# Weight loads and transposed pieces in the first feed-forward quarter of a transformer block on one core: another order in SyncE's queue, and one chunk of the next input split per block

## The chip, the cores and the metric

The kernel runs on one core of one Trainium2 chip. The metric is the device time of one execution in microseconds (us). The kernel before was timed three times: 1166.69, 1166.88 and 1167.59 us, a median of 1166.88 us. One more execution was taken by the hardware profiler; all rows quoted below are of that one, and their times count from its first instruction.

## What is computed

A pre-norm transformer block on x of 1 x 2048 x 448 in float32: grouped attention of 16 heads (width 28) with one key and value head, then a gated feed-forward of width 1792.

```python
x = A_x
h = x + _A_ref(_layernorm(x), A_wq, A_wk, A_wv, A_wo)   # attention
h2 = h + _B_ref(_layernorm(h), B_w1, B_w3, B_w2)
# _B_ref(x): gate = x @ w1; up = x @ w3; out = (silu(gate) * up) @ w2
```

## The kernel before

**Stages.** The rows of x are cut into four quarters of 512 (`NT = 4`). Attention runs up to 739 us of the span; from there the feed-forward runs quarter by quarter, and this text is about that. The order of all instructions on all engines is the order in which the program is written (a manual schedule); each engine then works through its own list strictly in turn, and semaphores make it wait where data are missing.

**A block.** One quarter t has 14 blocks k = 0 to 13 (`NF`), each for 128 of the 1792 hidden columns. The main loop (L1132 to L1169) does one block per pass. Weights and inputs are held as a high and a low part, so that three products of reduced precision stand for one in float32. From block (0, 4) on, a block on TensorE (PE) has four pieces in this order: the first half of the two input products of block k (`ffn1_half(..., 0)`), the first half of the w2 product of block k-1 (`ffn2_half(*prev, 0)`), the second half of the input products (`ffn1_half(..., 1)`), and the second half of the w2 product (in `rest`). All go through `two` (line L1025), two 64-row halves of the array at a time.

**Settling.** The two halves of the array change places between first and second half, so a PSUM bank that one has written is then written by the other. `settle` (L1029) keeps them apart: ScalarE (ACT) reads one element of the bank into `pexp`, and PE's next write of that bank waits for this read. In each block ACT does in this order: settle the input products' bank after the first half (PE's second half of the input products waits for it), settle the w2 product's bank (`pexp<-pb`), Silu (L1033), the high part of the hidden value (L1040), whatever `call(t, k)` holds, and the settle of the w2 product's second half (PE's next w2 product waits for it). What `call(t, k + 0.5)` holds comes after that settle and ahead of the next block.

**Weights.** `load_w13(k)` (L175 to L177) issues six DMAs on SyncE's (SP) queue for the columns of block k of w3 and w1, `load_w2(k)` (L184) one. They go to places that attention has left: `W13[6]`, `W13[7]` to `QR3`, `W13[8]`, `W13[9]` to `OT`, `W13[10]` to `W13[13]` to `OS`, the last rows of w2 to `WO`. `split_w(k + 2)` stands at the top of block k: VectorE (DVE) casts (L483), GpSimd (POOL) subtracts (L484). `split_w2(k + 1)` (L496, L497) stands behind the second half of the w2 product. DVE's list of one block is: cast of `W13[k+2]`, product with Silu (L1035), low part of the hidden value (L1041), work of `call(t, k)`, cast of `W2[k+1]`, work of `call(t, k + 0.5)`.

**The next quarter's input.** `ln_norm` and `blocks` (DVE, L213 and L225) norm 128 rows of the next quarter and transpose them in 32 x 32 blocks. What is left to reach the full transposed input is done by DMA: `blocks` puts 16 pieces per 128 rows into a list, and `move(m)` (L238) issues the next m of them on SP. A piece writes 32 partitions and 32 columns of all chunks c of the tile `xh` at once (`to[..., :m, ...]`, m of 4 or 3), so each chunk is whole only when all 64 pieces of a quarter have landed. `split_x(t, c)` (L243, L247) then makes the high and the low part of chunk c: a copy on ACT (two for c = 3) and a subtraction on DVE.

**Where the work stands.** `on(t, k, ...)` puts work into the table that `call` reads, from L1110 to L1129. In the first quarter before: 16 pieces behind block 1, the loads of `W13[8]` and `W13[9]` at 2, of `W13[6]` and `W13[7]` at 2.5, 16 pieces behind block 3, all other loads at 4.5, 16 pieces each behind blocks 5 and 7, chunks 0 and 1 split at 11, chunks 2 and 3 at 12.

Of the kernel before, what the change touches and what calls it, by code (L numbers as in the profile page):

```python
# [35 lines left out]
def block_kernel(  # L36
# [842 lines left out]
    for s in range(AHEAD, LAST):  # L879
        i, c = divmod(s, NC)  # L880
        n, kt = divmod(c, NQ)
# [221 lines left out]
    def on(t, k, fn, *args):  # L1103
        after.setdefault((t, k), []).append((fn, args))
# [10 lines left out]
    for n in range(NQ):  # L1115
        on(0, FULL - 1 + n // 2 / 2, wo_rows, tl, n)
        on(0, 8 + n, ln_stats, tl, n)
    on(0, 4.5, put_late)
    for k in range(8, NF):
        on(0, 2 if k < 10 else 4.5, load_w13, k)  # L1120
        on(0, 4.5, load_w2, k)
    on(0, 12, ln_rstd, tl)
    for t in range(1, NT):
        for n in range(NQ):
            on(t - 1, 1 + 2 * n, ln_norm, t, n)
            on(t - 1, 1 + 2 * n, blocks, t, n)
            on(t - 1, 1 + 2 * n, move, 16)
        on(t - 1, 11, split_x, t, 0, 1)
        on(t - 1, 12, split_x, t, 2, 3)  # L1129

    prev = None
    for t in range(NT):  # L1132
# [68 lines left out]
```

## Time and profile before

| | |
|---|---|
| median of the three runs | 1166.88 us |
| profiled execution: its time, its span | 1165.67 us, 1163.8 us |
| granted TensorE clock, mean | 1.000 |
| PE busy | 1149.7 us (99%) |
| DVE, ACT, POOL busy | 796.9, 765.0, 331.4 us |
| chain that ended last, PE's share | 87% |

A row of the timeline gives start, duration, engine, line, operation, what it writes `<-` what it reads, a count, and in brackets how long the engine had been idle and what ended that. A `q` behind an engine's name (SPq) is its queue of DMA issues: such a row tells of the issue, and the data land later. A row of the windows gives busy time and number of instructions of PE, PE's weight loads (PEld), DVE, ACT and POOL in that stretch, then the granted clock, the share of the DMA engines and GB/s.

### The profile page before, as it was taken

How to read it: one execution, taken by the hardware profiler on the slowest of the kernel's cores; microseconds unless marked ns; L12 is line 12 of the kernel's file. 1: busy time of each engine (PE TensorE's matmuls, PEld its weight loads, DVE VectorE, ACT ScalarE, POOL GpSimd, SP SyncE). 2: the span in 40 equal slices, each digit the busy share in tenths (PEclk: the TensorE clock that was granted, in tenths of full speed). 3: DMA queues.
4: the chain of work that ended last, by engine and by line, in shares of the span. 5: the costliest groups of instructions: out<-in, count | busy, mean ns of one | idle time of the engine just before them, and what ended most of it. 6: DMA issues, size and time to landing. Idle time of an engine off the chain costs nothing.

```text
span 1163.8 us, 25849 instructions
## 1 busy us (share of the span) xinstructions
PE 1149.7 (99%) x10154; PEld 765.9 (66%) x10154; DVE 796.9 (68%) x1498; ACT 765.0 (66%) x1587; POOL 331.4 (28%) x242
## 2 busy tenths in 40 slices
PE   8999999999999999999999999999999999999998
PEld 6664444445444445444445444688989999999997
DVE  8878999897899998999998982254443344334333
ACT  5649999996999997999997999512232232222221
POOL 5312001101101111110111012335465555556552
PEclk9999999999999999999999999999999999999999
DMA  4010100001000001110001100134101001100000
GB/s 167 10 37 1 34 12 18 19 16 46 19 14 8 19 24 38 31 24 11 10 23 44 29 19 19 54 85 124 27 34 18 16 1 43 17 7 33 1 2 32
DMA packets 67834, 34.51 MB, mean 30 GB/s; under 512 B 44672, under 2 KB 62336, under 8 KB 67712
## 3 DMA queue, kind: packets, MB, share of 16 engines
q1 hardware_dynamic: 67712, 32.86, 10.7%
q8 instruction: 80, 1.31, 0.5%
q14 instruction: 42, 0.34, 0.1%
HBM read 20.37 MB, written 3.80 MB: 21 GB/s over the span
## 4 chain that ended last, share of the span: by engine, by line
PE 87%; SPq 4%; ACT 3%; DVE 3%; issue 1%; DMA 1%; POOL 0%; ACTq 0%; DVEq 0%; POOLq 0%
PE po L424 21%; PE pb L408 20%; PE pa L1025 16%; PE pa L324 10%; PE pb L1025 8%; PE pa L166 4%; PE pb L166 4%; SPq L238 3%; PE po L1025 3%; DVE mx L334 1%; PE pb L1071 1%; ACT OT L431 1%; ACT ab L345 1%; PE pb L274 0%; DMA xh<-xn 0%
## 5 line engine op out<-in xcount | busy, mean ns | idle before, releaser
L334 DVE TENSOR_REDUCE mx<-pa 128x1 f32<-128x512 f32 x689 | 440.3, 685 | 22.0 <-PE pb L408 13.0
L408 PE MATMUL pb<-qs,KS 32*128 32x512 f32 x3072 | 384.8, 425 | 0.0
L415 ACT ACTIVATE pt<-pb 128x512 f32<-128x512 f32 x684 | 365.7, 619 | 19.9 <-PE pb L408 17.1
L408 PEld LDWEIGHTS pb<-qs,KS 32*128 32x128 f32 x3072 | 233.8, 182 | 133.1 <-ACT pt L415 66.9
L324 PE MATMUL pa<-KS,qs 32*128 32x512 f32 x886 | 311.5, 459 | 1.5 <-ACT ab L345 0.2
L324 PEld LDWEIGHTS pa<-KS,qs 32*128 32x128 f32 x886 | 138.5, 182 | 83.1 <-DVE mx L334 46.6
L1025 PE MATMUL pa<-xl,qs 64*128 64x512 f32 x1044 | 189.1, 388 | 0.0
L424 PE MATMUL po<-pt,VA 128*32 128x512 f32 x1368 | 182.2, 604 | 0.4 <-ACT pt L415 0.4
L1025 PE MATMUL pa<-xh,qs 64*128 64x512 f32 x739 | 153.6, 388 | 0.0
L455 POOL TENSOR_TENSOR OT<-OT,rb 128x512 f32<-128x512 f32 x15 | 19.7, 1312 | 458.1 <-DMA rb<-sd 202.1
L1025 PE MATMUL pb<-w2s,pt 64*128 64x448 f32 x1050 | 143.1, 361 | 3.8 <-ACT pexp L1029 2.6
L1035 DVE TENSOR_TENSOR pt<-pa,pt 128x512 f32<-128x512 f32 x49 | 33.9, 691 | 161.3 <-ACT pt L1033 155.2
L1025 PEld LDWEIGHTS pa<-xl,qs 64*128 64x128 f32 x1044 | 136.0, 184 | 5.0
L1025 PEld LDWEIGHTS pb<-w2s,pt 64*128 64x128 f32 x1050 | 121.3, 184 | 8.9 <-ACT pexp L1029 4.3
L352 DVE CUSTOM_DVE_ANT_0 ab<-pa,ab 128x512 f32<-128x512 f32 x138 | 93.6, 687 | 39.0 <-PE pa L324 34.4
L1025 PEld LDWEIGHTS pa<-xh,qs 64*128 64x128 f32 x739 | 103.6, 184 | 5.0
L415 ACT ACTIVATE xl<-pb 128x512 f32<-128x512 f32 x170 | 99.5, 609 | 9.1 <-PE pb L408 6.8
L415 ACT ACTIVATE xh<-pb 128x512 f32<-128x512 f32 x170 | 104.1, 630 | 0.0
L1033 ACT ACTIVATE pt<-pa 128x512 f32<-128x512 f32 x49 | 29.3, 599 | 94.9 <-PE pa L1025 90.9
L424 PE MATMUL po<-xh,VA 128*32 128x512 f32 x340 | 89.4, 605 | 0.0
L424 PE MATMUL po<-xl,VA 128*32 128x512 f32 x340 | 89.4, 605 | 0.0
L345 ACT ACTIVATE ab<-pa 128x512 f32<-128x512 f32 x138 | 82.2, 608 | 6.5 <-PE pa L324 4.9
(156 smaller groups left out, 1401.9 us busy)
## 6 DMA issues: line engine op xcount, KB each, us to landing
rb<-sd SPq DMA_DIRECT2D x64, 64.0 KB
QR<-OT SPq DMA_DIRECT2D x60, 56.0 KB
QR<-in_B_w_dram SPq DMA_DIRECT2D x16, 192.0 KB
X<-in_A_x_dram SPq DMA_DIRECT2D x3, 896.0 KB
out_dram<-X SPq DMA_DIRECT2D x3, 896.0 KB
xh<-xn SPq DMA_DIRECT2D x128, 16.0 KB
xh<-xn SPq DMA_DIRECT2D x128, 12.0 KB
w<-in_B_w_dram SPq DMA_DIRECT2D x8, 192.0 KB
```

The source lines that it names most:

```text
L166: pe.matmul(ps, lhs[b][:, cb, lsl], (rhs[2] if ca == 3 and len(rhs) == 3 else rhs[a])[:, ca, rsl], start=(k == 0), stop=(k == len(terms) - 1),
L238: sy.dma_start(*moves.pop(0))
L324: pe.matmul(ps, QS[i][r, 0, n * P : (n + 1) * P], KS[0][r, kt * T : (kt + 1) * T] if keys is None else keys[r], start=True, stop=True)
L334: ve.tensor_reduce(self.to(), ps, axis=AX.X, op=ALU.max)
L345: se.activation(self.ab, ps, AF.Relu)
L352: ve.tensor_tensor_reduce(self.ab, ps, self.ab, 1.0, -3.0e38, ALU.add, ALU.max, self.to())
L408: pe.matmul(self.ps, KS[k % 2][r, c * P : (c + 1) * P], QS[i][r, k // 2], start=(k == 0), stop=(k == 2))
L415: se.activation(f(PT[i, c, p][:, jj]), self.ps, AF.Exp, bias=0.0, scale=SCALE)
L424: pe.matmul(PO[i][32 * j : 32 * j + 32], VA[:, c], f(PT[i, c, j // 2][:, j % 2]), start=(c == 0), stop=(c == NC - 1))
L1025: pe.matmul(ps[:, : rhs.shape[-1]], lhs, rhs, start=bool(first), stop=bool(last), skip_group_check=True)
L1033: se.activation(sg, ps[0], AF.Silu)
L1035: ve.tensor_tensor(sg, ps[1], sg, op=ALU.mult)
```

## The change

In the first quarter the loads of `W13[8]` and `W13[9]` go from place 2 to 3.5, so that those of `W13[6]` and `W13[7]` come ahead of them; the other loads, all at 4.5 before, are spread over 4.5 to 7.5. The third and fourth 128 rows of the next quarter are normed and transposed behind blocks 4 and 6 (5 and 7 before), and their 32 pieces are issued seven at a time behind blocks 4 to 8. In the quarters 0, 1 and 2 chunk n of the next input is split at 9.5 + n, behind the w2 product, one chunk per block.

```diff
+    for k in (8, 9):
+        on(0, 3.5, load_w13, k)
     on(0, 4.5, put_late)
     for k in range(8, NF):
-        on(0, 2 if k < 10 else 4.5, load_w13, k)
-        on(0, 4.5, load_w2, k)
+        if k > 9:
+            on(0, k - 5.5, load_w13, k)
+        on(0, min(k - 3.5, 7.5), load_w2, k)
     on(0, 12, ln_rstd, tl)
     for t in range(1, NT):
         for n in range(NQ):
-            on(t - 1, 1 + 2 * n, ln_norm, t, n)
-            on(t - 1, 1 + 2 * n, blocks, t, n)
-            on(t - 1, 1 + 2 * n, move, 16)
-        on(t - 1, 11, split_x, t, 0, 1)
-        on(t - 1, 12, split_x, t, 2, 3)
+            k = (1, 3, 4, 6)[n] if t == 1 else 1 + 2 * n
+            on(t - 1, k, ln_norm, t, n)
+            on(t - 1, k, blocks, t, n)
+            if t > 1 or n < 2:
+                on(t - 1, k, move, 16)
+            on(t - 1, 9.5 + n, split_x, t, n)
+    for k in range(4, 9):
+        on(0, k, move, 7)
```

PE's list is the same in both. On SP, right behind the first 16 pieces (`xh<-xn`), the two loads into `QR3` (`W13[6]` and `W13[7]`, six DMAs each) come first now; the next 16 pieces follow them:

```order
 L238 DMA xh<-xn 32x4x32 x2
 L238 DMA xh<-xn 32x3x32 x2
+L175 DMA QR_91<-in_B_w_dram 128x3x128
+L176 DMA QR_91<-in_B_w_dram 64x128
+L177 DMA QR_91<-in_B_w_dram 64x128
+L175 DMA QR_91<-in_B_w_dram 128x3x128
+L176 DMA QR_91<-in_B_w_dram 64x128
+L177 DMA QR_91<-in_B_w_dram 64x128
```

Before, the twelve DMAs into `OT` stood here, and those into `QR3` behind them.

At the end of the first quarter's part of SP's list, just ahead of the store of the first quarter's result (`out_dram<-X`), before had the last weight load and then 32 pieces in a row, of which these are the first:

```order
L177 DMA w_1_11628<-in_B_w_dram 64x128
L184 DMA w_wo_11629<-in_B_w_dram 128x448
L238 DMA xh<-xn 32x4x32 x2
L238 DMA xh<-xn 32x3x32 x2
L238 DMA xh<-xn 32x4x32 x2
L238 DMA xh<-xn 32x3x32 x2
```

Now the loads of `W13[13]` and of the last rows of w2 stand between the pieces, and four pieces close the list:

```order
L238 DMA xh<-xn 32x3x32 x2
L184 DMA w_wo_11638<-in_B_w_dram 128x448
L184 DMA w_wo_11640<-in_B_w_dram 128x448
L175 DMA w_1_11639<-in_B_w_dram 128x3x128
L176 DMA w_1_11639<-in_B_w_dram 64x128
L177 DMA w_1_11639<-in_B_w_dram 64x128
L175 DMA w_1_11639<-in_B_w_dram 128x3x128
L176 DMA w_1_11639<-in_B_w_dram 64x128
L177 DMA w_1_11639<-in_B_w_dram 64x128
L184 DMA w_wo_11640<-in_B_w_dram 128x448
L238 DMA xh<-xn 32x4x32 x2
L238 DMA xh<-xn 32x3x32 x2
```

The number of issues in the quarter is the same: 64 pieces, eight loads of six DMAs, six loads of w2.

On ACT, before, the copies of chunks 0 and 1 stand behind the Silu (L1033) and the high part (L1040) of block 11, ahead of the settle of that block's w2 product (the next row) and of block 12's input products (the row after). The names in brackets are the queues whose DMAs the row waits for:

```order
L1033 ACTIVATE pt<-pa 128x512 [waits PE_49]
L1040 ACTIVATE pt<-pt 128x512 [waits DVE_49]
L243 ACTIVATE xl<-xh 128x512 [waits DMAHW4_49,DMAHW5_49,DMAHW3_49,DMAHW6_49,DMAHW2_49,DMAHW7_49,DMAHW1_49,DMAHW0_49]
L243 ACTIVATE xl<-xh 128x512
L1029 ACTIVATE pexp<-pb 1x1 [waits PE_49,Activation_49]
L1029 ACTIVATE pexp<-pa 1x1 [waits PE_49,Activation_49]
```

Now the copy of chunk 0 stands behind block 9's Silu, high part and last settle, and ahead of the settle of block 10's input products (`pexp<-po`):

```order
L1033 ACTIVATE pt<-pa 128x512 [waits PE_49]
L1040 ACTIVATE pt<-pt 128x512 [waits DVE_49]
L1029 ACTIVATE pexp<-pb 1x1 [waits PE_49,Activation_49]
L243 ACTIVATE xl<-xh 128x512 [waits DMAHW4_49,DMAHW5_49,DMAHW3_49,DMAHW6_49,DMAHW2_49,DMAHW7_49,DMAHW1_49,DMAHW0_49]
L1029 ACTIVATE pexp<-po 1x1 [waits PE_49,Activation_49]
L1029 ACTIVATE pexp<-pb 1x1 [waits PE_49,Activation_49]
L1033 ACTIVATE pt<-pa 128x512 [waits PE_49]
```

The chunks 1, 2 and 3 follow in the same place of blocks 10, 11 and 12. The wait on all eight queues moved two blocks up, with the copy that carries it.

## Prediction

> **What bounds the kernel now.** First the page: how much PE works, and what the chain that ended last is made of.
>
> ```profile
> PE 1149.7 (99%) x10154; PEld 765.9 (66%) x10154; DVE 796.9 (68%) x1498; ACT 765.0 (66%) x1587; POOL 331.4 (28%) x242
> PE 87%; SPq 4%; ACT 3%; DVE 3%; issue 1%; DMA 1%; POOL 0%; ACTq 0%; DVEq 0%; POOLq 0%
> ```
>
> PE is the bound; a change that leaves PE's list as it is can only win the places where PE stands, or make new ones. Second, the windows, to find these places in the feed-forward.
>
> ```profile
> 780.00:810.00 30.00, 28.03 (x254) 25.21 (x254) 12.34 (x21) 6.24 (x19) 13.84 (x7) 1.00 0.44 117
> 810.00:840.00 30.00, 28.62 (x262) 28.20 (x260) 12.50 (x25) 7.55 (x22) 15.35 (x8) 1.00 0.23 52
> 870.00:900.00 30.00, 30.00 (x278) 29.57 (x276) 11.74 (x21) 6.56 (x21) 16.36 (x9) 1.00 0.11 18
> ```
>
> The second number is PE's busy time: it stands in the first quarter and hardly anywhere behind it. Third, PE's timeline: first matmuls of blocks, and the rows with an idle time in brackets.
>
> ```profile
> 782.61 0.86 PE L1025 MATMUL pa<-xl,qs 64*128 64x512 f32 x6
> 786.06 0.47 PE L1025 MATMUL pb<-w2s,pt 64*128 64x448 f32 x2 [0.77 <-ACT pexp L1029]
> 787.74 1.29 PE L1025 MATMUL pb<-w2s,pt 64*128 64x448 f32 x10 [1.20 <-DVE pt L1041]
> ...
> 813.96 0.94 PE L1025 MATMUL pa<-xl,qs 64*128 64x512 f32 x6
> 821.16 0.39 PE L1025 MATMUL pa<-xl,qs 64*128 64x512 f32 x1
> 824.89 0.39 PE L1025 MATMUL po<-xl,qs 64*128 64x512 f32 x1
> 835.56 0.39 PE L1025 MATMUL po<-xl,qs 64*128 64x512 f32 x1
> 839.78 1.48 PE L1025 MATMUL pb<-w2s,pt 64*128 64x448 f32 x12 [1.38 <-ACT pexp L1029]
> 844.57 0.63 PE L1025 MATMUL pa<-xl,qs 64*128 64x512 f32 x4
> 852.29 0.39 PE L1025 MATMUL pa<-xl,qs 64*128 64x512 f32 x1
> 949.19 0.47 PE L1025 MATMUL po<-w2s,pt 64*128 64x448 f32 x1 [0.22 <-ACT pexp L1029]
> 954.03 0.86 PE L1025 MATMUL pa<-xl,qs 64*128 64x512 f32 x6
> 1050.97 1.48 PE L1025 MATMUL pb<-w2s,pt 64*128 64x448 f32 x12 [0.22 <-ACT pexp L1029]
> ```
>
> An undisturbed block takes 7.20 us (block 9 starts at 813.96, block 10 at 821.16). Block 5 starts at 782.61 and block 9 at 813.96, 31.35 for four blocks that need 28.80: block 5 loses **2.55**. Block 12 (835.56 to 844.57) loses **1.81**, block 13 (to 852.29, where the next quarter begins) **0.52**. The second quarter, 852.29 to 954.03, takes 101.74 for 14 blocks of 7.20, 0.94 too much, and the third has the same idle row near its end.
>
> **What the change removes.** Block 5's stall begins on DVE:
>
> ```profile
> 784.00 0.69 DVE L483 CAST qs<-QR 128x1024 fp32r<-128x1024 f32 x1 [7.99 <-DMA QR<-in_B_w_dram]
> ```
>
> The cast of `W13[6]` waits 7.99 for its load, and the product that block 4's hidden value needs is behind it. The loads into `QR3` are issued from 777.69 on (row below); now they come where the loads into `OT` began, at 770.37, 7.3 earlier. The cast then finds its data, and 2.55 go. The other stalls come from `split_x` on ACT:
>
> ```profile
> 820.26 0.60 ACT L1033 ACTIVATE pt<-pa 128x512 f32<-128x512 f32 x1 [2.07 <-PE pa L1025]
> 821.62 0.63 ACT L1040 ACTIVATE pt<-pt 128x512 fp32r<-128x512 f32 x1 [0.76 <-DVE pt L1035]
> 822.16 0.14 ACT L1029 ACTIVATE pexp<-pb 1x1 f32<-1x1 f32 x1
> 824.05 0.16 ACT L1029 ACTIVATE pexp<-po 1x1 f32<-1x1 f32 x1 [1.75 <-PE po L1025]
> ...
> 838.53 1.15 ACT L243 ACTIVATE xl<-xh 128x512 fp32r<-128x512 f32 x2 [1.82 <-DMA xh<-xn]
> 839.58 0.14 ACT L1029 ACTIVATE pexp<-pb 1x1 f32<-1x1 f32 x1
> 839.76 0.16 ACT L1029 ACTIVATE pexp<-pa 1x1 f32<-1x1 f32 x1
> ```
>
> The two copies of block 11 stand ahead of the settle at 839.58 that PE's w2 product of 839.78 waits for. In their new place they fall into ACT's gap between the last settle of a block (822.16) and the next settle (824.05), 1.75 idle: a copy is 0.6, chunk 3 has two, 1.25 (estimated from this row). So where the data are there, the copies cost nothing and the stalls of the blocks 12 and 13 go. On DVE the subtraction (one per chunk, as before) stands ahead of the next cast of weights, with a block's time left for it.
>
> **What it adds: a wait.** Chunk 0 is whole only with the last of 64 pieces, and its copy, which waits on all eight queues, moves from block 11 to block 9. When is the last piece there? SP:
>
> ```profile
> 758.93 11.39 SPq L238 DMA_DIRECT2D xh<-xn  x16
> ...
> 777.69 0.53 SPq L175 DMA_DIRECT2D QR<-in_B_w_dram  x1
> ...
> 785.44 10.64 SPq L238 DMA_DIRECT2D xh<-xn  x16
> ...
> 815.32 21.86 SPq L238 DMA_DIRECT2D xh<-xn  x32
> ```
>
> ```profile
> SPq L238 <- DVE pt L1041: 0.5, 1, 0.5
> ```
>
> ```profile
> 836.58 1.80 DMA xh<-xn
> ```
>
> From 758.93 to 837.18 SP issues 64 pieces, 48 parts of w13 loads and 6 of w2, 118 in 78.25 us, 0.66 each, and in all this time waits 0.5 for another engine (second fence). **SP is full, and the change reorders these 118 without dropping one.** The four pieces that close the new list are therefore issued up to the same 837.2, and the last lands 1.80 behind its issue, at 838.4 (third fence). The third and fourth rows' transposes are earlier by a block, but nobody waits for them.
>
> One thing can make it earlier: an issue that took longer.
>
> ```profile
> 825.04 2.50 SPq L238 DMA_DIRECT2D xh<-xn  x2
> ```
>
> Two pieces take 2.50 here instead of 1.24. If such a slow issue comes from PE's own progress (its instructions being fetched, say), it falls away while PE stands. So the landing lies between 837.2 and 838.4; I take the middle, **837.8**.
>
> ACT reaches the copy behind block 9's last settle, which with 2.55 won is at 819.6, and stands there 18 us. Behind it in ACT's list is the settle of block 10's input products; PE's second half of these products waits for it, at 824.89 - 2.55 = 822.34. The copy starts 0.15 behind the landing (838.53 against 838.38), the settle 0.53 behind that (half of 839.58 - 838.53), PE 0.20 later (839.78 - 839.58). PE goes on at 837.8 + 0.88 = 838.7 instead of 824.89 before. The 2.55 won in block 5 are thereby lost again: they only let PE reach the wait sooner. Weights due later (`W13[12]`, `W13[13]`) land by then under cover of this wait; without it they would be late (third rival).
>
> **PE's pace after the stand.** At its start:
>
> ```profile
> 1.36 4.20 PE L635 MATMUL po<-ident 128*128 128x128 f32 x20 [1.36 <-POOL ident masks.py:199]
> 7.14 0.66 PE L262 MATMUL pb<-ident,xn 128*128 128x128 f32 x4 [1.58 <-ACT xn L211]
> 7.63 1.28 PE L635 MATMUL po<-ident 128*128 128x128 f32 x10
> ```
>
> The first 20 matmuls take 4.20; at the pace of 7.63 (ten more cost 1.1) they would take 2.4. PE began slow and lost 1.8. After 1.58 idle (7.14) it was still fast. A stand of 16 us is not in this trace: the cost lies between 0 and 1.8, or twice that should the slow stretch last twice as long. I take 1.8, as 16 us are nearer to a start than to 1.58.
>
> [...]
>
> **The sum**, against the profiled execution:
> - PE's second half of block 10: 838.7 - 824.89 = +13.8.
> - Blocks 12 and 13 no longer stall: -1.81 - 0.52 = -2.3.
> - Ends of the second and third quarter: the excess is 0.94, of which about 0.1 also stands in undisturbed places; between 0.22 (the idle row) and 0.8 each. I take 0.65: -1.3. The pieces are in time there:
>
> ```profile
> 869.68 53.55 SPq L238 DMA_DIRECT2D xh<-xn  x64
> ```
>
> ```profile
> 925.50 0.14 ACT L1029 ACTIVATE pexp<-po 1x1 f32<-1x1 f32 x1
> ```
>
>   issued by 923.2, landed by 925.0, and ACT's settle of block 9, behind which the copy would stand, is at 925.50.
> - PE's pace: +1.8.
>
> Together **+12.0**: 1177.7 against the profiled 1165.67. The median of the runs is 1166.88, 1.2 above the profiled one, so for it 1178.9.
>
> **Rivals.**
> 1. *The wait, but full pace behind it.* As above without 1.8: 1177.1. For it speaks only the 1.58 of idle that cost nothing.
> 2. *The copy doesn't wait long, and the change is faster.* If the last piece landed by 821 or so (ACT's 819.6 and its 1.75 of idle), all stalls would go: -2.55 - 2.33 - 1.3 = -6.2, 1160.7. That decides at 821; SP would have to save 17 of its 78 us with the same 118 issues. Against it: the 0.66 per issue, and no wait on SP to be saved.
> 3. *No long wait, but late weights.* `W13[13]` is now issue 113 of 118: 758.93 + 113 x 0.66 = 833.9, landed near 836. Its cast must precede block 11's product with Silu, 6.9 behind the block's start (820.26 + 0.60 - 813.96), at 832.9: about 3 late, and -6.2 + 3 = -3.2, 1163.7. It needs rival 2's condition too.
> 4. *The change doesn't do what it says in block 5*, if the earlier load still came late: this would change nothing, since the wait in block 10 ends by SP's clock, not by PE's.
>
> **How the numbers follow.** Forecast 0.60: 1178.9, with the landing (837.2 to 838.4), the quarter ends (-0.4 to -1.6) and the pace (up to 3.6) between 1177 and 1182. Rival 1 0.28: 1175.5 to 1178.5. Rivals 2 and 3 0.04 each. The last 0.04 is shared by no change and something worse. The range 1174.5 to 1182.5 leaves out the rivals 2 and 3 and the rest, 0.12; it isn't cut closer, since the unknown costs fill it. About 0.2% (2.3 us) is what a measurement of this kernel can tell from no change. Slower by more than that: 0.60 + 0.28 + 0.02 = 0.90; faster 0.08; the same 0.02.
>
> **What would show it.** Right: one PE row in block 10's second half with some 16 us of idle behind ACT's settle, ACT's first L243 of the quarter released by DMA `xh<-xn` near 838, the DVE cast near 776 without its 7.99, no idle rows in blocks 5, 12, 13 or at 949 and 1051 (each moved by the loss), and about 25 matmul pairs of slower pace behind the stand. Wrong: a last piece that lands before 825, or ACT's copy in block 9 starting without a wait.

## The result, and the profile after

The changed kernel takes a median of **1178.93 us** (1178.61 to 1179.75), the kernel before, run beside it, 1167.24 us (1166.69 to 1169.27). The ratio is 1.0106, 95% interval 1.0094 to 1.0119: slower by about 1%. The profiled execution took 1178.61 us with a span of 1176.8 us and a mean granted clock of 0.993; the one of before took 1165.67 us. The difference between these two, 12.94 us, is what the following rows account for.

The page first: PE's row, the two rows of slices that changed, and the shares of the chain.

```profile
PE 1150.6 (98%) x10154; PEld 772.5 (66%) x10154; DVE 806.6 (69%) x1498; ACT 764.3 (65%) x1587; POOL 328.9 (28%) x242
PE   8999999999999999999999999999499999999998
PEclk9999999999999999999999999999799999999999
PE 85%; SPq 7%; DVE 2%; ACT 2%; DMA 1%; issue 1%; POOL 0%; ACTq 0%; DVEq 0%; POOLq 0%
```

PE's work is what it was (1149.7 before, 0.9 more now). One slice in forty, the 29th (it begins at 824), falls from 9 to 4, and in the same slice the clock falls to 0.7. In the chain SP's queue has 7% instead of 4%: SP has come onto the path. The timeline of PE in that place, after:

```profile
782.84 0.86 PE L1025 MATMUL pa<-xl,qs 64*128 64x512 f32 x6
786.56 0.86 PE L1025 MATMUL pa<-xl,qs 64*128 64x512 f32 x6
790.04 0.39 PE L1025 MATMUL pa<-xl,qs 64*128 64x512 f32 x1
...
818.84 0.39 PE L1025 MATMUL pa<-xl,qs 64*128 64x512 f32 x1
821.36 1.55 PE L1025 MATMUL pb<-w2s,pt 64*128 64x448 f32 x12
839.42 0.79 PE L1025 MATMUL po<-xl,qs 64*128 64x512 f32 x1 [16.51 <-ACT pexp L1029]
...
844.57 0.86 PE L1025 MATMUL pa<-xl,qs 64*128 64x512 f32 x6
866.17 0.39 PE L1025 MATMUL pa<-xl,qs 64*128 64x512 f32 x1
967.41 0.74 PE L1025 MATMUL pa<-xl,qs 64*128 64x512 f32 x4
1068.68 0.39 PE L1025 MATMUL pa<-xl,qs 64*128 64x512 f32 x1
```

Block 5 now takes 790.04 - 782.84 = 7.20: its stall is gone, since the cast of `W13[6]` on DVE finds its data and starts at 776.16 without a wait (before: 784.00, after 7.99 of waiting):

```profile
776.16 0.68 DVE L483 CAST qs<-QR 128x1024 fp32r<-128x1024 f32 x1
```

Blocks 6 to 9 follow at 7.20 (790.04 to 818.84 is four of them). In block 10 the first half of the w2 product runs at 821.36, and then PE stands **16.51** us until ACT's settle. The blocks 11, 12 and 13 take 844.57 to 866.17, three times 7.20: the stalls there are gone as well. What was to be won in this quarter was won, and one wait has eaten it. What PE waits for is in the chain of after, and what came ahead of that on ACT in ACT's timeline:

```profile
836.74 1.79 DMA xh<-xn
...
838.68 0.04 ACT xl L243
...
839.22 0.15 ACT pexp L1029
...
839.42 0.79 PE po L1025
```

```profile
819.87 0.14 ACT L1029 ACTIVATE pexp<-pb 1x1 f32<-1x1 f32 x1
838.68 0.63 ACT L243 ACTIVATE xl<-xh 128x512 fp32r<-128x512 f32 x1 [18.68 <-DMA xh<-xn]
```

From the last issue on SP, at 836.74, the chain leads through the landing at 838.53 to the copy of chunk 0 on ACT, the settle behind it and PE. ACT had been ready at 820.0 and waited 18.68 for the last of 64 pieces. Behind the stand PE is slow; the windows of after (the number after POOL's is the granted clock):

```profile
822.00:838.00 16.00, 0.91 (x10) 0.52 (x6) 0.69 (x3) 0.00 (x0) 1.13 (x1) 0.62 0.48 132
840.00:842.00 2.00, 2.00 (x12) 1.59 (x10) 0.64 (x2) 0.00 (x0) 1.28 (x1) 0.50 0.03 8
842.00:844.00 2.00, 2.00 (x18) 1.64 (x18) 0.00 (x0) 0.44 (x1) 1.09 (x1) 0.80 0.00 0
846.00:848.00 2.00, 2.00 (x22) 1.74 (x20) 1.97 (x6) 0.28 (x2) 0.52 (x1) 1.00 0.00 0
```

PE is busy all the time in 840 to 842 and gets 12 matmuls done where it gets 22 in 846 to 848: the clock is 0.50 against 1.00. Cut into stretches of 0.4 us, 822 to 846 of this run shows a clock of 1.00 or 0.50 in all but two of them: 0.65 in 825.60 to 826.00, which is 0.28 us of half clock, and 0.52 in 842.40 to 842.80, which is 0.38. So the half clock began near 825.7 and ended near 842.8.

### The profile page after: what moved, and what is told of

It reads as the page before. It is cut to its first block, busy times and chain, and to the rows that moved or that the text cites. A ratio compares the mean times of both kernels' runs of the same rounds, so it can differ in the third digit from the quotient of the medians.

```text
span 1176.8 us, 25851 instructions
## 1 busy us (share of the span) xinstructions
PE 1150.6 (98%) x10154; PEld 772.5 (66%) x10154; DVE 806.6 (69%) x1498; ACT 764.3 (65%) x1587; POOL 328.9 (28%) x242
## 3 DMA queue, kind: packets, MB, share of 16 engines
q8 instruction: 80, 1.31, 0.5%
## 4 chain that ended last, share of the span: by engine, by line
PE 85%; SPq 7%; DVE 2%; ACT 2%; DMA 1%; issue 1%; POOL 0%; ACTq 0%; DVEq 0%; POOLq 0%
PE po L424 20%; PE pb L408 19%; PE pa L1025 16%; PE pa L324 10%; PE pb L1025 8%; PE pb L166 4%; SPq L238 4%; PE po L1025 4%; PE pa L166 3%; SPq L177 1%; SPq L175 1%; ACT OT L431 1%; SPq L176 1%; ACT ab L345 1%; DVE mx L334 1%
## 5 line engine op out<-in xcount | busy, mean ns | idle before, releaser
L1025 PE MATMUL pa<-xl,qs 64*128 64x512 f32 x1044 | 193.6, 389 | 0.0
L1025 PE MATMUL pa<-xh,qs 64*128 64x512 f32 x739 | 157.6, 389 | 0.0
L1025 PE MATMUL pb<-w2s,pt 64*128 64x448 f32 x1050 | 143.2, 360 | 0.0
L1025 PEld LDWEIGHTS pa<-xl,qs 64*128 64x128 f32 x1044 | 140.2, 185 | 3.2
L1025 PEld LDWEIGHTS pb<-w2s,pt 64*128 64x128 f32 x1050 | 123.1, 184 | 2.4 <-DVE pt L1041 0.4
L1025 PEld LDWEIGHTS pa<-xh,qs 64*128 64x128 f32 x739 | 106.7, 185 | 3.1
L1033 ACT ACTIVATE pt<-pa 128x512 f32<-128x512 f32 x49 | 29.3, 597 | 96.9 <-PE pa L1025 92.8
```

The costliest lines, as they stand in the source:

```text
L1025: pe.matmul(ps[:, : rhs.shape[-1]], lhs, rhs, start=bool(first), stop=bool(last), skip_group_check=True)
L1033: se.activation(sg, ps[0], AF.Silu)
```

## The experiments

The theory is that of the prediction: SP's list of 118 issues sets when chunk 0 is whole, the copy's place ahead of a settle makes PE stand until then, and the restart runs slowly for a few us. Against it stand three others: that the new order on SP (later weights, pieces between them) is what costs; that the stand is due to the number of pieces or of bytes and not to the number of issues; and that the pace behind the stand has another cause than the stand.

**Only the split moved.** The kernel before, with its order on SP, and chunk n of the next input split at 9.5 + n:

```diff
-        on(t - 1, 11, split_x, t, 0, 1)
-        on(t - 1, 12, split_x, t, 2, 3)
+        for n in range(NQ):
+            on(t - 1, 9.5 + n, split_x, t, n)
```

> The kernel before with only split_x moved (chunk n at 9.5 + n in every quarter); SyncE's order is that of before. Theory of the wait (ScalarE stands on chunk 0 until the last of 118 issues has landed): the same list lands its last piece near 838.4, TensorE goes on near 839.4 in block 10, the clock drops once, and the time is that of the change, 1177.5 to 1180, with block 5's stall back but without effect on the end. Rival theory of the order (the interleaved weight loads and pieces cost the time): with the old order nothing is lost, 1164 to 1167.

Measured: 1179.65 us (1176.92 to 1181.29), ratio 1.0108 (1.0087 to 1.0129). PE, ACT and SP of this run:

```profile
789.04 1.29 PE L1025 MATMUL pb<-w2s,pt 64*128 64x448 f32 x10 [1.20 <-DVE pt L1041]
840.21 0.79 PE L1025 MATMUL po<-xl,qs 64*128 64x512 f32 x1 [13.74 <-ACT pexp L1029]
```

```profile
839.48 0.63 ACT L243 ACTIVATE xl<-xh 128x512 fp32r<-128x512 f32 x1 [15.88 <-DMA xh<-xn]
```

```profile
817.49 20.64 SPq L238 DMA_DIRECT2D xh<-xn  x32
```

Block 5's stall is back (first row), so PE comes to the gate later and stands 13.74 instead of 16.51; it leaves it 0.79 later than in the changed kernel (840.21 against 839.42), as SP's last piece comes 0.79 later. That piece is issued up to 838.13 in this order and to 837.34 in the new one; SP's list itself began 1.08 later here (760.46 against 759.38). The time is the same within the intervals: the moved split alone makes the loss, and no part of the new order on SP in it can be seen.

**Only the order on SP.** The change, with the splits back at 11 and 12:

```diff
-            on(t - 1, 9.5 + n, split_x, t, n)
+        on(t - 1, 11, split_x, t, 0, 1)
+        on(t - 1, 12, split_x, t, 2, 3)
```

> The change with split_x back at its old places (chunks 0 and 1 at 11, 2 and 3 at 12); SyncE's new order stays. Theory of the wait: no stand of 16 us. Block 5 wins 2.5, but W13[13], now issue 113 of 118, lands near 837 and holds VectorE in block 11, and with it the copies ahead of the settle: some 5 lost in block 12 where 1.8 was lost before. Together within 2 of the kernel before, 1165 to 1169. Rival theory of the order: 1177 to 1180.

Measured: 1166.30 us (1164.45 to 1167.47, ten runs), ratio 0.9996 (0.9987 to 1.0006): no change. Its PE and DVE:

```profile
831.55 1.27 PE L1025 MATMUL pb<-w2s,pt 64*128 64x448 f32 x10 [1.22 <-DVE pt L1041]
841.15 1.48 PE L1025 MATMUL pb<-w2s,pt 64*128 64x448 f32 x12 [2.33 <-ACT pexp L1029]
```

```profile
827.79 0.69 DVE L483 CAST qs<-w 128x1024 fp32r<-128x1024 f32 x1 [3.29 <-DMA w<-in_B_w_dram]
837.09 0.69 DVE L483 CAST qs<-w 128x1024 fp32r<-128x1024 f32 x1 [3.04 <-DMA w<-in_B_w_dram]
```

The 2.55 of block 5 are won here too (it takes 791.04 - 783.84 = 7.20), and lost again at the end of the quarter, so that from block 5 to the next quarter it is 69.79 us (783.84 to 853.63) where before took 69.68 (782.61 to 852.29): the casts of `W13[12]` and `W13[13]` now wait 3.29 and 3.04 for their loads, DVE's later work is pushed back, and PE stands 1.22 in block 11 and 2.33 in block 12. SP's time is only dealt out otherwise. In the changed kernel these late weights hide behind the long stand, as the prediction had it; it named both, though its third rival worked out `W13[13]` alone.

**PE kept busy through the stand.** The change, and in block 10, ahead of the second half, 130 matmuls of 128 x 128 into a bank:

```diff
+                if (t, k) == (0, 10):
+                    fill = bank()
+                    for _ in range(130):
+                        pe.matmul(fill[:, :P], ident, ident, start=True, stop=True)
+                    done(fill)
                 ffn1_half(t, k, W, ps, 1)
```

> The change with 130 matmuls of 128 x 128 (0.11 us each, into a bank that nobody reads) put between the first w2 half and the second half of the input products of block 10, so that TensorE works through 14 of the 16.5 us of its stand. If the pace behind the stand costs 1.7 (the slow stretch), the granted clock stays at 1.00 and the time falls to 1177.2, or to 1178.3 if fetching the added instructions delays SyncE by 1.1. If the slow pace costs nothing, it stays at 1178.9 or above.

Measured: 1189.82 us (1189.76 to 1190.08), ratio 1.0197 (1.0180 to 1.0215). The time missed its expectation because the filling was too long: such a matmul in float32 stands as two records of about 0.11 us in the trace, so 130 of them took 29 us (823.2 to 852.2) and not half of that. The pace behind them could be read all the same (a window of this run):

```profile
852.00:854.00 2.00, 2.00 (x19) 1.70 (x19) 0.00 (x0) 0.00 (x0) 0.00 (x0) 1.00 0.04 8
```

With no stand ahead the second half runs at a clock of 1.00. A second run has 62 matmuls, which end ahead of the wait:

> As the run with 130 added matmuls, with 62 of them: a 128 x 128 float32 matmul showed as two records of 0.11 us, so 62 fill 13.8 us of the stand of 16.5 and end ahead of the wait. If the pace behind the stand costs 1.7, the granted clock stays at 1.00, block 10's second half to block 11 takes 3.5 in place of 5.15, and the time falls to 1177 (1176.5 to 1178). If it costs nothing, the time stays at 1178.9 or above.

Measured: 1178.56 us (1176.42 to 1179.28), ratio 1.0098 (1.0081 to 1.0115). PE, the windows and SP:

```profile
840.99 0.50 PE L1025 MATMUL po<-xl,qs 64*128 64x512 f32 x1 [2.62 <-ACT pexp L1029]
844.60 0.86 PE L1025 MATMUL pa<-xl,qs 64*128 64x512 f32 x6
```

```profile
822.00:838.00 16.00, 16.00 (x145) 15.69 (x143) 1.25 (x4) 0.00 (x0) 1.13 (x1) 1.00 0.48 131
842.00:844.00 2.00, 2.00 (x21) 1.69 (x18) 0.21 (x1) 0.40 (x1) 1.71 (x1) 1.00 0.03 8
```

```profile
825.62 5.44 SPq L238 DMA_DIRECT2D xh<-xn  x7
```

PE stands 2.62 instead of 16.51, the clock stays at 1.00, and from the second half to block 11 it takes 844.60 - 840.99 = 3.61 instead of 844.57 - 839.42 = 5.15: **1.54 of the changed kernel's loss is the pace, and the stand is its cause.** The mean clock says the same of every execution: 0.999 or 1.000 in the four with 62 matmuls, 0.992 or 0.993 in the four of the changed kernel. The time does not show it: 1178.56 lies above the range expected for a gain (1176.5 to 1178) and just below what was expected without one (1178.9). The trace says why for the profiled execution: PE left the gate at 840.99 and not at 839.42, 1.57 later. SP's list began 1.42 later (760.80 against 759.38), and the list itself took 0.16 more; in it one of the seven pieces from 825.62 on was slow (5.44; without a slow one seven take 4.5, below). So the pace is shown by the traces and not resolved by the time.

**Fewer issues, the same pieces.** The change, with loads drawn together: the last 64 rows of w3 and of w1 for two blocks at once, the rows of w2 of four or two blocks in one DMA. 98 issues instead of 118, and the same 64 pieces and the same bytes:

```diff
+    def load_pair(k):
+        both = FL[k].rearrange("p (j c m e) -> p j c m e", j=2, c=4, m=2)
+        for m, w in enumerate((w3, w1)):
+            for j in range(2):
+                cols = slice((k + j) * P, (k + j + 1) * P)
+                sy.dma_start(both[:, j, 0:3, m], w[0:384, cols].rearrange("(c p) e -> p c e", p=P))
+            last = w[384:448, k * P : (k + 2) * P].rearrange("p (j e) -> p j e", j=2)
+            for r in (0, 64):
+                sy.dma_start(both[r : r + 64, :, 3, m], last)
...
+    for k, at_k in ((8, 4.5), (12, 6.5)):
+        on(0, at_k, load_w2_rows, k, min(4, NF - k))
+    for k, at_k in ((10, 4.5), (12, 6.5)):
+        on(0, at_k, load_pair, k)
```

> The change with fewer issues on SyncE for the same data: the last 64 rows of w3 and w1 are loaded for two blocks at once, w2's rows 8 to 11 and 12 to 13 in one issue each; 98 issues in place of 118. Theory of the wait: the last piece lands 20 x 0.66 = 13 earlier, near 825.5, and TensorE goes on near 826.5, 4 behind its normal time in block 10; the time falls by 13, and by 1.7 more if the clock stays up: 1164.5 to 1167.5. If the wait isn't set by the count of issues: above 1172.

Measured: 1167.88 us (1166.17 to 1171.98, ten runs), ratio 1.0014 (1.0003 to 1.0025), a median 0.4 above the expected range. The lines stand 15 further down in this kernel (L1040 is L1025 of the others). SP, PE and the windows:

```profile
818.24 7.08 SPq L253 DMA_DIRECT2D xh<-xn  x11
```

```profile
827.44 0.50 PE L1040 MATMUL po<-xl,qs 64*128 64x512 f32 x1 [4.42 <-ACT pexp L1044]
```

```profile
827.00:829.00 2.00, 1.56 (x10) 1.23 (x12) 1.29 (x2) 0.55 (x3) 0.26 (x1) 0.72 0.03 8
829.00:831.00 2.00, 2.00 (x12) 1.62 (x10) 0.00 (x0) 0.00 (x0) 2.00 (x1) 0.50 0.00 0
831.00:833.00 2.00, 2.00 (x20) 1.74 (x18) 0.69 (x1) 0.62 (x2) 0.11 (x1) 0.92 0.00 0
```

The last issue ends at 825.32 instead of 837.34, 12.0 earlier for 20 fewer issues, 0.60 for each, and PE's stand is shorter by the same 12 (4.42 for 16.51). Pieces and bytes are the same, so it is the number of issues on SP, each piece being one, that sets the landing. The remaining loss is the rest of the stand and a restart that is still slow: the clock is 0.50 in 829 to 831. It halved near 827.9, just behind the restart, and was back near 831.3: an estimate from the 0.72 and 0.92 of these rows, if the clock had no other values than 0.50 and 1.00 in this run either.

**The copies put where the pieces have landed.** The kernel before, with the order of the two pairs of loads from the change, the later quarters' splits at 9.5 + n, and in the first quarter all four chunks behind block 12's w2 product:

```diff
-        on(0, 2 if k < 10 else 4.5, load_w13, k)
+        on(0, 3.5 if k < 10 else 4.5, load_w13, k)
...
-        on(t - 1, 11, split_x, t, 0, 1)
-        on(t - 1, 12, split_x, t, 2, 3)
+        for n in range(NQ):
+            on(t - 1, 12.5 if t == 1 else 9.5 + n, split_x, t, n)
```

> The kernel before with W13[6] and W13[7] loaded ahead of W13[8] and W13[9] (these at 3.5), and with split_x behind the w2 product: all four chunks of the first quarter at 12.5, one chunk per block at 9.5 + n in the later quarters. Theory of the wait: the last piece lands at 838.4, before ScalarE comes to the copies (841.5), so no wait; block 5 wins 2.5, blocks 12 and 13 win 2.3, the five copies in one gap cost about 1.3, the later quarters win 0.9: 4.5 below the kernel before, 1161.5 to 1164. Rival theory of the place (a copy behind the last settle and ahead of the next block's settle costs by itself): no gain over 1167.

Measured: **1160.95 us** (1160.87 to 1161.49), ratio 0.9951 (0.9936 to 0.9966), a little better than expected. SP and ACT:

```profile
816.28 21.50 SPq L238 DMA_DIRECT2D xh<-xn  x32
```

```profile
842.48 1.66 ACT L243 ACTIVATE xl<-xh 128x512 fp32r<-128x512 f32 x3
```

SP is done at 837.78, as late as ever, but ACT now comes to the copies at 842.48 and waits for nothing. PE has no idle row in the rest of the quarter; only block 13 takes 0.6 longer, as five copies stand ahead of its settles. The pieces are as late as before; what cost the time was a copy that ACT reaches ahead of the landing, with settles behind it that PE waits for.

**Both.** Fewer issues, and the first quarter's chunks split at 10.5, 11.5, 12.5 and 12.5:

```diff
-            on(t - 1, 9.5 + n, split_x, t, n)
+            on(t - 1, min(10.5 + n, 12.5) if t == 1 else 9.5 + n, split_x, t, n)
```

> As the run with 98 issues, and the chunks of the first quarter split one block later (10.5, 11.5, and 2 and 3 at 12.5). Theory of the wait: ScalarE comes to chunk 0 at 827, behind the last landing near 825.5, so no stand at all; against the kernel before, block 5 wins 2.5, blocks 12 and 13 win 2.3, the later quarters 0.9: 1160.5 to 1162.5. Rival theory of the place (copies behind the last settle cost by themselves): 1165 or more.

Measured: **1160.64 us** (1160.14 to 1162.62), ratio 0.9954 (0.9940 to 0.9969). The copy begins right behind its settle, without a wait (ACT):

```profile
827.95 0.61 ACT L258 ACTIVATE xl<-xh 128x512 fp32r<-128x512 f32 x1
```

It is not to be told from the kernel ahead of it: where the copies wait for nothing, no gain from 20 issues fewer on SP can be seen. Both beat the kernel before by about 0.5%.

## Why the prediction was right

It forecast 1178.9, and the median is 1178.93; that they agree to 0.03 is chance, as two errors of 0.9 cancel. The sum was made against the profiled execution and gave 12.0 where that shows 12.94. The 1.2 by which the median of before stood above its profiled run was then added for after as well, where median and profiled run lie only 0.3 apart. Term by term, in us (SP's and PE's rows of after are the sources, with those of before in the prediction):

| step | predicted | measured |
|---|---|---|
| PE's second half of block 10 | +13.8 | 839.42 - 824.89 = +14.53 |
| blocks 12 and 13 | -2.3 | -2.33 |
| pace behind the stand | +1.8 | 5.15 - 3.48 = +1.67 |
| ends of the second and third quarter | -1.3 | -0.96 |
| sum | +12.0 | +12.91 |

3.48 is the same stretch of block 5, 786.56 to 790.04. The start of the last quarter moved from the row below (of before, PE) to 1068.68, by 12.92.

```profile
1055.76 0.39 PE L1025 MATMUL pa<-xl,qs 64*128 64x512 f32 x1
```

*The gate.* Its 0.7 too little is all in the landing, 838.53 where 837.8 was taken; copy, settle and PE follow it by 0.15, 0.54 and 0.20, as worked out. That SP is full and its list is as long as before decided the case, and the rows of after show it once more:

```profile
759.38 11.31 SPq L238 DMA_DIRECT2D xh<-xn  x16
...
795.91 1.66 SPq L177 DMA_DIRECT2D OT<-in_B_w_dram  x1
...
806.44 5.64 SPq L238 DMA_DIRECT2D xh<-xn  x7
816.25 4.56 SPq L238 DMA_DIRECT2D xh<-xn  x7
824.97 4.52 SPq L238 DMA_DIRECT2D xh<-xn  x7
834.75 2.59 SPq L238 DMA_DIRECT2D xh<-xn  x4
```

From 759.38 to 837.34 it is 77.96 us for 118 issues, 0.66 each as before (78.25). The guess about the slow issue was right in kind: the one at 825 of before has gone, and no issue behind 822, while PE stands, is slow. But it brought only 0.3, since the slow ones ahead of it (in the rows 1.66 and 5.64) were slower than before's, and SP's list began 0.45 later. So the range for the landing (837.2 to 838.4) was missed by 0.1, because it took the start of SP's list as fixed.

*Block 5* won its 2.55 and lost them at the gate: the run with the moved split alone, where they aren't won, ends as late. This is shown, not argued. *Blocks 12 and 13* came out to the digit. *The quarter ends* gave 0.50 (101.24 for 101.74) and 0.46 (101.27 for 101.73), near the middle of their range (0.22 to 0.8) and below the 0.65 taken: the idle rows went, and about 0.45 above 14 blocks of 7.20 stays in each quarter. *The pace* came within 0.13, but this is in part luck. Its 1.8 was taken from PE's slow start. There the profile of before gives a granted clock of 1.00 (row below), though the trace's first clock record begins only at 4.96, so that the two have one cause is not shown:

```profile
2.00:4.00 2.00, 2.00 (x11) 2.00 (x11) 0.59 (x3) 0.22 (x2) 0.00 (x0) 1.00 0.87 283
```

In the run with the split alone the same wait cost 3.0 behind the restart (last section), still inside the 0 to 3.6 that the prediction allowed.

Of the rivals the first (full pace) is refuted by the clock of 0.50 and by the runs with PE kept busy. The second and third needed a landing before 821; it came at 838.53, and even 20 issues fewer bring it only to 826.5 (issued at 824.72, 1.80 to land), so the gate still closes for 4.42. The third's late weights are real, as the run with the order alone shows; its 832.9 should have been 832.7 (block 11 starts at 813.96 + 14.40 - 2.55 = 825.81), which changes nothing. The fourth didn't come: block 5 does take 7.20. Wrong in a detail was "about 25 matmul pairs of slower pace": PE's rows of half pace are eight pairs, most of them 0.43 apart instead of 0.23.

## What to carry to other kernels

Before a copy that waits for a transfer is moved forward in an engine's list, look at what stands behind it in that list: an instruction of 0.14 us (here a settle of one element) turns the copy's wait into a stand of the engine that sets the end, 16.51 us here. SP's queue, which issued without a pause (in before it waited 0.5 us in all for another engine), took 78.25 us for its 118 issues in the old order and 77.96 in the new: reordering hardly moved its last item. Fewer issues (0.6 us each here) and a consumer that comes later both helped; to put all pieces ahead of the late weights, so that these are last, was not tried. A stall that is removed ahead of such a gate (2.55 us in block 5) is given back at the gate, so add up the gains behind it and not ahead of it.

## What the runs showed of the hardware

**How long the half clock lasted.** It lasted from about 825.7 to 842.8 in the changed kernel, 17.1 us, and from about 827.9 to 831.3 in the run with fewer issues, 3.4 us. In the run with the split alone it lasted from about 829.4 to 846.4, 17.1 us, an estimate made as that for the run with fewer issues (0.73 over 16 us is 8.6 us of it, 0.89 over 2 us is 0.44):

```profile
822.00:838.00 16.00, 4.47 (x42) 4.09 (x38) 2.43 (x5) 0.84 (x3) 1.23 (x2) 0.73 0.15 23
846.00:848.00 2.00, 2.00 (x18) 1.73 (x18) 1.30 (x3) 1.31 (x3) 0.00 (x0) 0.89 0.00 0
```

The cost to the matmuls behind the restart was 1.67 in the first, 1.7 in the second (5.18 instead of 3.48 from the second half to block 11), and 3.0 in the run with the split alone (6.47). So a stand of 4.42 already paid, while one of 2.62 did not (the clock stayed at 1.00), and the price in these traces is 1.7 to 3.0.

What differs is how much of the half clock lay behind the restart. It ended 3.4 behind it in the changed kernel (842.8 against 839.42) and 6.2 behind it in the run with the split alone (846.4 against 840.21); in the run with fewer issues, where it began 0.5 behind the restart (827.44), all of its 3.4 lay there. The price is about half of that each time. Why it went on longer in the run with the split alone is not shown; no run varied it by itself. In the ten executions of the run with fewer issues the time goes with the mean clock: four with 0.999 took 1166.2 to 1166.7 us, five with 0.997 took 1167.7 to 1168.4, and one with 0.993 took 1172.0.

**Slow issues on SP come together with instruction packets.** With PE at work an issue on SP took 0.5 to 1.1 us longer about every 14 us (781.99, 795.91 and 809.74 in the changed kernel), and in each of these stretches one packet of 16 KB of the kind "instruction" moved; in 822 to 838 of the changed kernel, with PE standing, there was neither, and with the 62 matmuls added both were back (5.44 for seven pieces). The page of the profile of after has 80 such packets and 1.31 MB of them, beside PE's 10154 matmuls and 10154 weight loads: one packet for 254 of these on average. PE runs 278 matmuls and 276 weight loads in the 30 us from 870 on (before), so 254 of them in about 13.8, an estimate that is close to the 14 between slow issues. On PE's own rows nothing of it is seen, as blocks 5 to 9 keep their 7.20; on SP's issues it is. That the packets belong to PE, and that they make the issues slow, was not tried by itself.
